# A table of tokens kept in SBUF and filled by matmuls instead of by indirect DMAs, in an attention and mixture-of-experts kernel

## The chip, the cores and the metric

The kernel runs on one core of a Trainium2 chip. The metric is the device time of one execution in microseconds (us), as the median of several runs. The core has a matrix engine, TensorE (PE, with its weight loads shown apart as PEld), and VectorE (DVE), ScalarE (ACT), GpSimd (POOL) and SyncE (SP, which issues most DMAs). Each engine takes its instructions in the order in which the program lists them.

## The reference

Block-causal attention, and then a mixture of experts on its output: each token goes to the expert with the largest logit and its output is scaled by that expert's probability.

```python
def _attn_ref(q, k, v):                       # batch 8, heads 8, seq 576, head_dim 64
    scores = scale * np.matmul(q, k.transpose(0, 1, 3, 2))
    mask = block_i >= block_j                 # blocks of 64 positions
    scores = np.where(mask, scores, -1000000000.0)
    scores = scores - np.max(scores, axis=-1, keepdims=True)
    attn = np.exp(scores)
    attn = attn / (np.sum(attn, axis=-1, keepdims=True) + 1e-09)
    return np.matmul(attn, v)

def _moe_ref(x, expert_emb, tau, w1, w2):     # x: 4608 tokens x 512, 8 experts, hidden 1024
    logits = xn @ en.T / tau                  # rows of x and expert_emb, each over its norm
    expert_idx = np.argmax(logits, axis=1)
    probs = softmax(logits)
    for e in range(E):
        mask = expert_idx == e
        h = np.maximum(x[mask] @ w1[e], 0.0)
        out[mask] = gate_w[mask, None] * (h @ w2[e])
```

## The kernel before, in words

**Attention.** Two heads make a pair; 8 batches of 4 pairs give 32 pairs, `n`. The 576 positions are five row tiles (`NJ` = 5: four of 128 and one of 64). A pair goes through `prep` (transposes of `kn` and `qn`, L326, split into a rounded part `kh`, `qh` and a remainder `kl`, `ql`, L343 and L345), `maxes` (scores for the row maxima, L361 on PE, L367 on DVE; then `nmr`, L374, which PE transposes), `scores` (four matmuls per group, L422, and the exponential on ACT, L429, into `pT` and `pA`; partial row sums on POOL, L400 to L403), `values` (L457), `sums` (L476 to L502, ends in the copy `su`) and `post` (transposes of `oe` and `su`, division, the tokens' rows `xrow` and their logits `lgh`). Several pairs are in flight at once.

**The order of the work** is written out by hand. A string of letters for each pair, in FIRST, STEADY and FINAL, says which part takes its next step: s scores, v values and sums, f post, m maxes, p prep, l loads, r the router. `run()` (L866) reads the string; each letter moves one generator to its next `yield`. So a generator with more steps spreads over more letters, and what follows it comes later. Four PSUM tiles of two banks each (`banks`, L196) go round: `take_bank` takes the one that was given back longest ago, `give_bank` puts one at the end.

**The router.** When a batch's four pairs are done, `route(b)` (L587) finds each token's expert (`ohb`, a one-hot), its rank among the tokens of that expert (matmuls with a triangle of ones, L616 to L620), and for all but the last batch its place in a table of [expert, row of 128 slots, lane]: `table_rows` (L740). The table lies in DRAM. Five indirect DMAs a batch on GpSimd's queue (L672) write 128 token numbers each, 4 bytes to a place:

```python
w = nc.gpsimd.indirect_dma_start(
    out=table, out_offset=bass.IndirectOffsetOnAxis(ap=rowj[:, j:j + 1], axis=0),
    in_=tokf[:, b, j:j + 1], in_offset=None, ...)
```

The table is set to zero at the start by a DMA (L284) and read back by two: `early_rows` (L711) reads the two rows of the early slots when batch 5 (`EB`) is routed, and `tbt` (L1243) reads all of it after the attention part.

**The MoE part** works on slots of 128 tokens of one expert. Weights are streamed and split into rounded part and remainder; each product is three matmuls (L1122). Two early slots of expert 0 begin while the last pairs of attention end (L1238 to L1386): there the four double banks are given up and smaller PSUM pools take their place. `free_bank` (L197) is the double bank that holds the transposed tokens of the early slots, and the new pools are opened in the order `ps_b`, `ps_m1`, `ps_e`.

## Time and profile before

| | |
|---|---|
| median of 3 runs | 811.11 us (809.23 to 811.66) |
| profiled execution | 810.42 us, its span 808.7 us |
| granted TensorE clock | 1.000 of full speed over the span (2.4 GHz) |
| busy share of the span | PE 96%, PEld 78%, DVE 75%, ACT 50%, POOL 54% |
| instructions | PE 7160, DVE 1382, ACT 831, POOL 420 |
| DMA | 93.95 MB in 141421 packets, 118925 of them under 512 bytes |

The span runs from the first instruction to the last; attention fills about the first 350 us, MoE the rest. In a row of the timeline the first number is the start, the second the duration; the bracket at the end says how long the engine had been idle before it and what ended that idle time ("issue": nothing that the profile shows). A row with a count of several instructions gives the time from the first one's start to the last one's end; where matmuls follow each other closely, that includes the latency of the last.

### The profile page before, as it was taken

How to read it: one execution, taken by the hardware profiler on the slowest of the kernel's cores; microseconds unless marked ns; L12 is line 12 of the kernel's file. 1: busy time of each engine (PE TensorE's matmuls, PEld its weight loads, DVE VectorE, ACT ScalarE, POOL GpSimd, SP SyncE). 2: the span in 40 equal slices, each digit the busy share in tenths (PEclk: the TensorE clock that was granted, in tenths of full speed). 3: DMA queues.
4: the chain of work that ended last, by engine and by line, in shares of the span. 5: the costliest groups of instructions: out<-in, count | busy, mean ns of one | idle time of the engine just before them, and what ended most of it. 6: DMA issues, size and time to landing. Idle time of an engine off the chain costs nothing. (4 is left out here: it accounts for less than half of the span.)

```text
span 808.7 us, 23043 instructions
## 1 busy us (share of the span) xinstructions
PE 779.2 (96%) x7160; PEld 627.3 (78%) x7160; DVE 604.2 (75%) x1382; ACT 408.4 (50%) x831; POOL 435.7 (54%) x420
## 2 busy tenths in 40 slices
PE   8999999999999998899999999999999999999997
PEld 3678878787878776668878887788888888888885
DVE  6667878686868776658868777877887778877881
ACT  2566757575757564664744456553533332543222
POOL 7555676767676757772347288784761111661110
PEclk9999999999999999999999999999999999999999
DMA  4745364545454543163845357454441111111111
GB/s 104 169 95 136 84 158 105 147 104 132 101 140 100 141 100 101 29 231 127 297 151 166 100 158 235 152 167 150 148 153 45 55 54 45 38 49 55 54 35 39
DMA packets 141421, 93.95 MB, mean 116 GB/s; under 512 B 118925, under 2 KB 120541, under 8 KB 141260
## 3 DMA queue, kind: packets, MB, share of 16 engines
q1 hardware_dynamic: 133228, 69.74, 31.2%
q0 software_dynamic: 8032, 22.36, 8.7%
q8 instruction: 66, 1.08, 0.6%
q14 instruction: 95, 0.78, 0.3%
HBM read 72.71 MB, written 19.71 MB: 114 GB/s over the span
## 5 line engine op out<-in xcount | busy, mean ns | idle before, releaser
L1175 DVE STREAM_TRANSPOSE pt<-h 32x256 f32<-32x256 f32 x528 | 240.6, 456 | 31.3 <-ACT h L1149 14.1
L367 DVE TENSOR_REDUCE nmx<-psm 128x16 f32<-128x1024 f32 (+2 forms) x128 | 125.6, 986 | 21.4 <-PE psm L361 18.5
L912 POOL TENSOR_TENSOR ring_l<-raw,ring_h 128x1024 f32 (+1 forms) x49 | 116.3, 2406 | 35.7 <-ACT ring_h L907 20.0
L1189 POOL DMA_INDIRECT out_dram<-y,outi x36 | 36.7, 1020 | 176.5 <-ACTq L1061 118.8
L1122 PE MATMUL py<-ring_h,hh 128*128 x272 | 109.3, 402 | 0.7 <-ACT h L1149 0.7
L1122 PE MATMUL py<-ring_l,hh 128*128 x272 | 106.3, 391 | 0.0
L429 ACT ACTIVATE pT<-psm 128x640 f32<-128x640 f32 (+2 forms) x128 | 89.1, 703 | 28.2 <-PE psm L361 16.8
L403 POOL TENSOR_TENSOR pS<-pS,pT 128x640 f32<-128x640 f32 (+2 forms) x93 | 93.5, 1006 | 10.9 <-ACT pT L431 3.2
L1122 PE MATMUL py<-ring_h,hl 128*128 x272 | 88.8, 389 | 0.0
L1122 PE MATMUL ph<-ring_l,xh 128*128 x280 | 86.3, 390 | 0.8 <-POOLq L1073 0.8
L1122 PE MATMUL ph<-ring_h,xh 128*128 x280 | 86.3, 389 | 0.6 <-ACTq L1061 0.6
L457 PE MATMUL psm<-pT,vo 128*64 128x320 f32 (+2 forms) x640 | 76.1, 380 | 1.0 <-issue 1.0
L1188 ACT ACTIVATE y<-py,xg 128x512 f32<-128x512 f32 x34 | 23.4, 689 | 103.5 <-PE py L1122 97.9
L1183 DVE TENSOR_TENSOR hl<-pt,hh 128x512 fp32r<-128x512 f32 x66 | 42.5, 686 | 42.0 <-ACT hh L1181 42.0
L422 PE MATMUL psm<-qh,kh 64*128 64x320 f32 (+4 forms) x384 | 66.5, 341 | 5.9 <-ACT pT L429 3.5
L907 ACT CAST ring_h<-raw 128x1024 f32 (+1 forms) x62 | 61.0, 1050 | 22.1 <-POOLq L1073 11.6
L1181 ACT CAST hh<-pt 128x512 fp32r<-128x512 f32 x66 | 35.5, 590 | 72.1 <-DVE pt L1175 71.7
L1122 PE MATMUL ph<-ring_h,xl 128*128 x280 | 69.2, 389 | 0.0
L457 PEld LDWEIGHTS psm<-pT,vo 128*64 128x64 f32 x640 | 43.2, 137 | 29.3 <-issue 1.9
L1122 PEld LDWEIGHTS ph<-ring_l,xh 128*128 128x128 f32 x280 | 52.5, 188 | 12.1 <-POOLq L1073 1.2
L1122 PEld LDWEIGHTS ph<-ring_h,xh 128*128 128x128 f32 x280 | 52.5, 188 | 11.7 <-ACTq L1061 0.8
L1122 PEld LDWEIGHTS ph<-ring_h,xl 128*128 128x128 f32 x280 | 52.6, 188 | 10.9
(289 smaller groups left out, 1680.7 us busy)
## 6 DMA issues: line engine op xcount, KB each, us to landing
raw<-in_moe_w_dram SPq DMA_DIRECT2D x60, 512.0 KB
qn<-in_q_dram SPq DMA_DIRECT2D x64, 128.0 KB
kn<-in_k_dram SPq DMA_DIRECT2D x64, 128.0 KB
vo<-in_v_dram SPq DMA_DIRECT2D x64, 128.0 KB
xbuf<-xrow SPq DMA_DIRECT2D x28, 260.0 KB
raw<-in_moe_w_dram POOLq DMA_DIRECT2D x4, 512.0 KB
qa<-nmT SPq DMA_DIRECT2D x64, 2.5 KB
xbuf<-xrow SPq DMA_DIRECT2D x7, 130.0 KB
```

Source lines behind the costliest of these rows:

```text
L367: nc.vector.tensor_reduce(m[:, :, f:f + o // w], mt[:, :, 0:o].rearrange("p h (b c) -> p h b c", c=w), axis=AX.X, op=ALU.max, negate=True)
L403: nc.gpsimd.tensor_tensor(o, o, pT[:, :, off[t]:off[t] + w], op=ALU.add)
L422: nc.tensor.matmul(st[0:kw, hh, o:o + c1 - c0], kk[hd[hh], t * P:t * P + kw], qq[hd[hh], 64 + c0:64 + c1], start=(x == 0), stop=(x == len( ...
L429: nc.scalar.activation(pT[:, :, f:f + w] if c0 else pA, st[:, :, 0:w], AF.Exp, scale=scale)
L457: m = nc.tensor.matmul(ob[hh * D:(hh + 1) * D, b0:b0 + q1 - c0], rows(vo, ends_v, n, t)[:, hh, :], pTs[hh][0][:, f0:f0 + q1 - c0] if c0 el ...
L907: return (nc.scalar.copy if eng is nc.scalar else eng.tensor_copy)(piece(ring_h, to, c, half), raw[i][:, c * CW:(c + 1) * CW])
L912: return eng.tensor_tensor(piece(ring_l, to, c, half), raw[i][:, c * CW:(c + 1) * CW], piece(ring_h, to, c, half).bitcast(F32), op=ALU.sub ...
L1122: m = nc.tensor.matmul(out, ac, slots[g]["w", i](r, c * n + off), start=(u == 0 and c == 0), stop=(c == nk - 1 and u == len(turns) - 1))
L1175: nc.vector.transpose(pt[32 * j:32 * j + 32, :, 32 * i:32 * i + 32], h[32 * i:32 * i + 32, :, j, :])
L1181: nc.scalar.copy(sets["hh"][u], pt[:, 4 * u:4 * u + 4])
L1183: nc.vector.tensor_tensor(sets["hl"][u], pt[:, 4 * u:4 * u + 4], sets["hh"][u].bitcast(F32), op=ALU.subtract)
L1189: nc.gpsimd.indirect_dma_start(out=out, out_offset=bass.IndirectOffsetOnAxis(ap=to, axis=0), in_=y, in_offset=None, bounds_check=NT - 1, o ...
```

## The change

The table moves to SBUF as `tbt` [128 lanes, 8 experts, rows], and the indirect DMAs, the zeroing DMA and the two reads of the table go. For each token tile two tables are made: `lane` [128 tokens, 128 lanes], by two ScalarE activations (the square of lane minus the token's lane, then Relu(token - token x square), which leaves the token's number at its lane and 0 elsewhere), and `inrow` [128 tokens, 8 x rows], on GpSimd as the product of the one-hot of the expert and the one-hot of the row. Five matmuls, with `lane` as weights and `inrow` moving, add up in a bank of PSUM, and DVE adds them to `tbt`. The rows counted are `rb` = 5, 9, 14, 18, 23, 27, 32 in batches 0 to 6, so `inrow` is 40 to 256 wide.

For batches 0 to 5 the route begins six router letters later; the subtraction of the largest logit moves from GpSimd to DVE, and the squares for the norms (ACT) are issued among the first router steps. `reserve` is written into `route`. The banks are numbered anew, and at the hand-over the pools are opened in the order `ps_m1`, `ps_e`, `ps_b`; the last pools of the MoE part are opened in another order as well. Four router letters of FINAL's fourth string go, the squares of pairs 29 and 30 are both put off to the end, and the first weight pieces are rounded in turn by GpSimd and ScalarE.

```diff
-    "rfvfsrrrmrrsmrfvfmrrrrsrrmsvmrvvrrvvrrsrrfrfrvfrrrsfvvfrsvvfvvrvrfrr",
+    "rfvfsrrrmrrsmrfvfmrrrrsrrmsvmrvvvvsrrfrfrvfrrrsfvvfrsvvfvvrvrfrr",
...
     banks = [ps_m.tile([P, 2, 512], F32, name=f"psm{i}") for i in range(4)]
-    free_bank = banks[2]
+    banks = [banks[i] for i in (2, 1, 3, 0)]
+    free_bank = banks[0]
...
-        nc.gpsimd.dma_start(table.rearrange("(c p t) o -> p c (t o)", p=RC, t=P),
-                            zcol[0:RC, 0:NCH * P].rearrange("p (c t) -> p c t", t=P))
+        nc.gpsimd.memset(tbt, 0.0)
...
+        def square(j):
+            if b <= EB:
+                squares(xrow[:, j, 0:DM], ss[:, j:j + 1])
+
+        if b <= EB:
+            for _ in range(6):
+                yield
         nc.vector.tensor_reduce(lg, lgh.rearrange("p j h e -> p j e h"), axis=AX.X, op=ALU.add)
         yield
         nc.vector.tensor_reduce(mx, lg, axis=AX.X, op=ALU.max)
         yield
-        eng.tensor_tensor(lg, lg, bc(mx.unsqueeze(2), P, NJ, E), op=ALU.subtract)
+        (nc.vector if b <= EB else eng).tensor_tensor(lg, lg, bc(mx.unsqueeze(2), P, NJ, E), op=ALU.subtract)
...
-            t2 = above(rk, ebase)
+            t2 = sm.tile([P, NJ, E], F32, name="t2")
+            nc.vector.tensor_tensor(t2, rk, ohb, op=ALU.mult)
...
         if b < B - 1:
+            here = inrow[:, :, 0:E * rb]
             for j in range(NJ):
-                w = nc.gpsimd.indirect_dma_start(
-                    out=table, out_offset=bass.IndirectOffsetOnAxis(ap=rowj[:, j:j + 1], axis=0),
-                    in_=tokf[:, b, j:j + 1], in_offset=None, bounds_check=E * RE * P - 1, oob_is_err=False)
...
+                nc.scalar.activation(away, pio, AF.Square, bias=place[:, 0, j:j + 1])
+                nc.gpsimd.tensor_tensor(here[:, j].rearrange("p (e r) -> p e r", e=E),
+                                        bc(ohb[:, j].unsqueeze(2), P, E, rb),
+                                        bc(rowhot[:, j:j + 1, 0:rb], P, E, rb), op=ALU.mult)
+                yield
+                nc.scalar.activation(lane[:, j], away, AF.Relu, bias=tokf[:, b, j:j + 1], scale=tokn[:, b, j:j + 1])
                 if (b == B - 2 or j == NJ - 1) and pieces:
                     store_piece()
                 yield
+            for _ in range(8 if b >= EB else 3):
+                yield
+            bank = take_bank()
+            new = bank[:, 0, 0:E * rb]
+            for j in range(NJ):
+                nc.tensor.matmul(new, lane[:, j], here[:, j], start=(j == 0), stop=(j == NJ - 1))
+            nc.vector.tensor_tensor(tbt[:, :, 0:rb], tbt[:, :, 0:rb], new.rearrange("p (e r) -> p e r", e=E), op=ALU.add)
+            give_bank(bank)
+            yield
...
     def early_rows():
-        et = rt.tile([P, EARLY], F32, name="et")
+        et = tbt[:, 0, 0:EARLY]
         none = rt.tile([P, EARLY], F32, name="enone")
-        nc.sync.dma_start(et, table.rearrange("(p r) o -> p (r o)", p=P)[:, 0:EARLY])
...
-    def table_rows(t, ohb):
+    def table_rows(t, rb):
...
-        nc.gpsimd.tensor_tensor(t, t, ohb, op=ALU.mult)
+        rowt = sm.tile([P, 2, NJ], I32, name="rowt")
+        place = sm.tile([P, 2, NJ], F32, name="place")
         yield
         nc.vector.tensor_reduce(rowj, t, axis=AX.X, op=ALU.max)
         yield
...
+        nc.vector.tensor_scalar(place, rowt, -1.0, None, op0=ALU.mult)
+        nc.vector.tensor_tensor(rowhot[:, :, 0:rb], bc(minus[:, 0:rb].unsqueeze(1), P, NJ, rb),
+                                bc(place[:, 1].unsqueeze(2), P, NJ, rb), op=ALU.is_equal)
...
     ring(0)
-    tbt = st.tile([P, NCH * RC], F32, name="tbt")
-    nc.sync.dma_start(tbt, table.rearrange("(p r) o -> p (r o)", p=P))
...
     banks.remove(free_bank)
+    banks[1:] = banks[:0:-1]
...
+    ps_m = pool(psum_t, "ps_m1", 4, space=PSUM, reuse_waits="tile")
+    ps_e = pool(psum_t, "ps_e", 1, space=PSUM, reuse_waits="tile")
     ps_b = pool(psum_t, "ps_b", 1, space=PSUM, reuse_waits="tile")
-    ps_m = pool(psum_t, "ps_m1", 4, space=PSUM, reuse_waits="tile")
```

How this moves instructions is seen in the order on single engines. In the names, `psm_147` to `psm_153` are the double banks of PSUM; a number names one tile within one kernel only, here and for `kh`, `qh`, `kl`, `ql`, `qa` and `pT`. The lines L326 to L502 of before are seven higher after the change. The first place is PE in the pair after a batch has been routed. Before, the 320-wide scores follow the last maxes and take the bank of the earlier 320-wide scores (psm_152), whose exponential is done:

```order
L422 MATMUL psm_150<-qh_183,kh_189 128x448 x2
L422 MATMUL psm_150<-ql_186,kh_189 128x448 x2
L422 MATMUL psm_150<-qh_183,kl_192 128x448 x2
L422 MATMUL psm_150<-qa_195,ka 128x448 x2
L361 MATMUL psm_151<-kh_190,qh_184 128x64 x2
L422 MATMUL psm_152<-qh_183,kh_189 128x320 x2
L422 MATMUL psm_152<-ql_186,kh_189 128x320 x2
L422 MATMUL psm_152<-qh_183,kl_192 128x320 x2
L422 MATMUL psm_152<-qa_195,ka 128x320 x2
L326 MATMUL psm_153<-ident,kn_157 128x64 x8
```

After, the five lane matmuls stand between:

```order
L429 MATMUL psm_149<-qh_180,kl_189 128x448 x2
L429 MATMUL psm_149<-qa_192,ka 128x448 x2
L711 MATMUL psm_148<-inrow,lane 128x144 x5
L368 MATMUL psm_150<-kh_187,qh_181 128x64 x2
L429 MATMUL psm_147<-qh_180,kh_186 128x320 x2
L429 MATMUL psm_147<-ql_183,kh_186 128x320 x2
L429 MATMUL psm_147<-qh_180,kl_189 128x320 x2
L429 MATMUL psm_147<-qa_192,ka 128x320 x2
L333 MATMUL psm_148<-ident,kn_154 128x64 x8
```

They take a bank of the round (psm_148), the maxes behind them the next one (psm_150), and the 320-wide scores the bank that was used by the earlier maxes of 192 and 320 columns (psm_147), which DVE reduces.

The second place is ACT in the same pair. Before, the cast of `kh` and one exponential lie between the 448-wide exponential and the copy of the sums:

```order
L429 ACTIVATE pA<-psm_152 128x512
L429 ACTIVATE pT_212<-psm_153 128x2x320
L429 ACTIVATE pT_212<-psm_152 128x2x448
L343 CAST kh_190<-psm_151 128x2x5x64
L429 ACTIVATE pT_212<-psm_153 128x2x320
L502 COPY su_206<-psm_150 128x192
L379 CAST nmT<-psm_153 10x128
L429 ACTIVATE pT_212<-psm_152 128x2x192
```

After, the lane tables of the batch stand among them:

```order
L702 ACTIVATE lane<-away,tokf,tokn 128x128
L697 ACTIVATE away<-pio,place 128x128
L436 ACTIVATE pT_217<-psm_148 128x2x448
L702 ACTIVATE lane<-away,tokf,tokn 128x128
L350 CAST kh_186<-psm_149 128x2x5x64
L697 ACTIVATE away<-pio,place 128x128
L436 ACTIVATE pT_217<-psm_150 128x2x320
L702 ACTIVATE lane<-away,tokf,tokn 128x128
L697 ACTIVATE away<-pio,place 128x128
L509 COPY su_202<-psm_147 128x192
L386 CAST nmT<-psm_150 10x128
L436 ACTIVATE pT_217<-psm_148 128x2x192
```

Between the cast of `kh` and the copy `su` there are three more activations of 128x128, and three more ahead of the cast.

The third place is DVE in the pair in which a batch's route begins. Before, the first router steps stand ahead of the `ql` subtraction (L345) and among the reductions of the maxes (L367):

```order
L594 TENSOR_REDUCE lg<-lgh 128x40
L596 TENSOR_REDUCE mx<-lg 128x5
L345 TENSOR_TENSOR ql_186<-psm_150,qh_183 128x2x5x64
L601 SCALAR_TENSOR_TENSOR t_2116<-lg,erev 128x40
L367 TENSOR_REDUCE nmx_200<-psm_153 128x2x8
L371 MEMSET nmx_200 64x2x2
L603 TENSOR_REDUCE mx<-t_2116 128x5
L367 TENSOR_REDUCE nmx_200<-psm_150 128x2x8
L371 MEMSET nmx_200 64x2x2
L605 TENSOR_TENSOR hot_110<-t_2116,mx 128x40
L367 TENSOR_REDUCE nmx_200<-psm_153 128x2
L607 MEMSET hot_110 64x4
```

After, four of them stand together behind the last of these reductions and ahead of `nmr` (L374, after the change L381):

```order
L374 TENSOR_REDUCE nmx_197<-psm_148 128x2x8
L378 MEMSET nmx_197 64x2x2
L374 TENSOR_REDUCE nmx_197<-psm_147 128x2
L611 TENSOR_REDUCE lg<-lgh 128x40
L613 TENSOR_REDUCE mx<-lg 128x5
L615 TENSOR_TENSOR lg<-lg,mx 128x40
L618 SCALAR_TENSOR_TENSOR t_2889<-lg,erev 128x40
L381 TENSOR_REDUCE nmr_199<-nmx_197 128x10
```

The subtraction `lg<-lg,mx` is a DVE instruction now; before, it stood in POOL's queue.

## Rows read from the trace of the kernel before

**Rows 1.** The page: busy us (share of span) x instructions, by engine
```profile
PE 779.2 (96%) x7160; PEld 627.3 (78%) x7160; DVE 604.2 (75%) x1382; ACT 408.4 (50%) x831; POOL 435.7 (54%) x420
```

**Rows 2.** Windows: us, busy us (instructions) of PE, PEld, DVE, ACT, POOL; clock, DMA, GB/s
```profile
700.00:750.00 50.00, 50.00 (x231) 41.38 (x230) 40.51 (x85) 18.73 (x36) 21.94 (x16) 1.00 0.17 53
```

**Rows 3.** Groups of instructions by line and shape: busy us, mean ns, idle before
```profile
L672 POOL DMA_INDIRECT table<-tokf,rowj x35 | 35.2, 1005 | 9.9 <-issue 9.5 <-ACT oe L463 0.2
...
L400 POOL TENSOR_TENSOR pS<-pA,pT 128x256 f32<-128x256 f32 x31 | 22.7, 732 | 65.4 <-ACT pT L429 65.4
...
L582 ACT ACTIVATE xs<-xrow 128x128 f32<-128x128 f32 x20 | 6.2, 311 | 2.6 <-DVE xrow L538 2.1
```

**Rows 4.** Timeline, batch 2's route: start, duration, instruction, idle before and its releaser
```profile
183.52 0.42 PE L361 MATMUL psm<-kh,qh 64*128 64x192 f32 x4
...
184.25 0.47 PE L422 MATMUL psm<-qh,kh 64*128 64x448 f32 x2 [0.31 <-issue]
...
184.91 0.97 POOL L672 DMA_INDIRECT table<-tokf,rowj  x1 [0.30 <-issue]
...
185.86 1.55 DVE L367 TENSOR_REDUCE nmx<-psm 128x16 f32<-128x1024 f32 x2 [1.93 <-PE psm L361]
...
185.87 0.41 PE L422 MATMUL psm<-qh,kh 64*128 64x320 f32 x2 [0.52 <-ACT pT L429]
...
187.14 0.47 PE L326 MATMUL psm<-ident,kn 64*128 64x64 f32 x8 [0.43 <-DVE nmx L367]
```

**Rows 5.** Timeline, PE: first transposes of `kn` in three more pairs
```profile
175.88 0.40 PE L326 MATMUL psm<-ident,kn 64*128 64x64 f32 x8
...
197.44 0.46 PE L326 MATMUL psm<-ident,kn 64*128 64x64 f32 x8 [0.30 <-DVE nmx L367]
...
207.37 0.46 PE L326 MATMUL psm<-ident,kn 64*128 64x64 f32 x8 [0.19 <-DVE nmx L367]
```

**Rows 6.** Timeline of the pair before batch 3's route, four instructions
```profile
194.91 2.48 DVE L367 TENSOR_REDUCE nmx<-psm 128x16 f32<-128x1024 f32 x2
...
196.31 0.39 PE L422 MATMUL psm<-qh,kh 64*128 64x320 f32 x2
...
199.19 0.33 ACT L502 COPY su<-psm 128x192 f32<-128x192 f32 x1
...
199.65 0.29 PE L326 MATMUL psm<-ident,su 64*128 64x64 f32 x4
```

**Rows 7.** Timeline, router steps of two batches with the sums on POOL
```profile
207.36 0.19 DVE L605 TENSOR_TENSOR hot<-t,mx 128x40 bf16<-128x40 f32 x1
...
207.95 0.24 PE L619 MATMUL psm<-hot,onesb 128*128 128x32 bf16 x4
...
208.27 1.58 POOL L401 TENSOR_TENSOR pS<-pT 128x640 f32<-128x640 f32 x1
...
209.80 0.27 PE L326 MATMUL psm<-ident,nmr 64*128 64x64 f32 x2
...
336.26 1.54 POOL L401 TENSOR_TENSOR pS<-pT 128x640 f32<-128x640 f32 x1
...
336.64 1.23 DVE L605 TENSOR_TENSOR hot<-t,mx 128x40 bf16<-128x40 f32 x1
```

**Rows 8.** Timeline, PE: end of the attention part and the early slots
```profile
308.52 0.55 PE L457 MATMUL psm<-pT,vo 128*64 128x192 f32 x4 [0.96 <-issue]
...
311.12 0.50 PE L361 MATMUL psm<-kh,qh 64*128 64x448 f32 x4 [1.03 <-issue]
...
338.05 0.19 PE L616 MATMUL psm<-hot,triS 128*128 128x40 bf16 x1 [0.93 <-DVE hot L607]
...
347.61 0.48 PE L422 MATMUL psm<-qh,kh 64*128 64x448 f32 x2
...
349.61 0.34 PE L326 MATMUL psm<-ident,su 64*128 64x64 f32 x4
...
360.05 0.50 PE L1122 MATMUL psm<-ring_h,xh 128*128 128x512 f32 x1 [0.79 <-DVE hl L1101]
```

More of the change, by code (lines that the diff above doesn't have):

```diff
@@ L628, in route @@
             give_bank(rb)
+        square(4)
         yield
@@ L653, in route @@
         if b < B - 1:
-            rowj = yield from table_rows(t2, ohb)
+            rb = -(-(b + 1) * S // P)
+            place = yield from table_rows(t2, rb)
         nc.vector.reciprocal(ss, ss)
@@ L685 @@
     early_g = []
-    writes, ends = [], []
+    ends = []
     ei = st.tile([P, 2, EARLY], I32, name="ei")
@@ L1279 @@
     split_lo(0, 3, 0)
-    late.pop()()
+    for f in late:
+        f()
     for c in range(NPC):
```

65 lines of the change are left out of this document (32 added, 33 removed).

## The prediction

> **What bounds the kernel now.** I read the busy shares first: TensorE (PE) is busy 96% of the span, VectorE (DVE) 75%, ScalarE (ACT) 50%, GpSimd (POOL) 54% [rows 1]. In the MoE part PE has no idle time, 50.00 of 50 us [rows 2], so nothing can be won there but by taking PE work away, and the change touches none of it. What can move is the attention part, where PE stops for short waits; each counts in full if no later wait shrinks with it. So I looked, in the timeline of single instructions, for PE waits near what the diff removes, then for the slack of the instructions beside which it puts new work.
>
> What goes is 35 indirect DMAs, each 1.0 us of GpSimd [rows 3]. GpSimd has room, so that time is worth nothing by itself. But around the issues PE waits, though its producers are done. In batch 2's route the maxes of L361 start at 183.52 and last 0.42, so they end at 183.94; the reduction of them on DVE starts at 185.86 and its row names those maxes as releaser of a 1.93 wait. PE stands 0.31 ahead of the 448-wide scores (releaser "issue"), 0.52 ahead of the 320-wide ones, 0.43 ahead of the `kn` transposes: 1.26 in all, while POOL issues these DMAs, the last of the three from 184.91 to 185.88 [rows 4]. From `kn` to `kn` that pair takes 187.14 - 175.88 = 11.26 us, the next 197.44 - 187.14 = 10.30, the one after 207.37 - 197.44 = 9.93 [rows 4, 5]. I read this as: while such a DMA is issued, signals between the other engines come late.
>
> **The change part by part**, against the profiled execution's own 810.42 us (0.7 below the median of the runs, 811.11).
>
> *Removed DMAs, batches 0 to 4.* Bounds per batch: nothing, if other waits fill the holes, and 1.7 (both pairs over the undisturbed 9.93: 1.33 + 0.37). The waits say 1.26, the neighbouring pair 0.96. I take 1.1: 5 x 1.1 = 5.5 us gained.
>
> *Batch 5.* Two waits with releaser "issue", 0.96 at 308.52 and 1.03 at 311.12 [rows 8], go: 2.0 (bounds 0 and 2.0).
>
> *Batch 6*, the last with a table, issues its five while little runs. The last 448-wide score group stretches from 347.61 to 349.61, 2.00 us [rows 8]; four streams of 448 columns at the rate of 512 in 50/231 = 0.216 [rows 2] are 4 x 0.19 = 0.76. So 1.2, and 0.7 for the rest of its five issues, at 1.1/5 each: 1.9 (bounds 0 and 2.6).
>
> *PSUM of the early slots.* At 360.05 PE waits 0.79 for a DVE subtraction that reads `free_bank` [rows 8]: the new pool of maxes' tiles begins on that bank. With the new order a bank that was free longer lies there: 0.8 (0 to 0.8). What is late next is the loaded weight half, which I can't see there; hence the lower end.
>
> *The one-hot's wait.* At 338.05 the rank matmuls wait 0.93 for the one-hot [rows 8], because its DVE operation took 1.23 instead of 0.19 and ended when the sum on POOL that ran since 336.26 ended [rows 7]. Batch 6 keeps its order, with other neighbours: I take half, 0.5 (0 to 0.9).
>
> Gains: 5.5 + 2.0 + 1.9 + 0.8 + 0.5 = 10.7.
>
> *Products on POOL.* 35 products of 40 to 256 elements. L400, 256 elements wide, takes 0.73 [rows 3]; so they are shorter than the 1.0 of the DMA each replaces. POOL gets lighter: 0.
>
> *Lane matmuls.* 7 x 5 on PE, which hides nothing. Nearest below: four 128-row matmuls of 32 to 8 columns together 0.24 [rows 7]; nearest above: 512 columns, 0.216 each [rows 2]. So between 0.24 and 1.08 a batch. With 40 to 256 columns I take 0.3. They also take a bank out of the round of four. As the order shows, the 320-wide scores behind them then need a bank that the reductions from 194.91 to 197.39 still hold, while today they start at 196.31 [rows 6]: 1.1 later, less the 0.30 that `kn` waits today [rows 5], the matmuls themselves and the earlier maxes. I add 0.2: 7 x 0.5 = 3.5 (bounds 7 x 0.24 = 1.7 and 7 x (1.08 + 0.8) = 13).
>
> *Lane tables on ACT.* 70 activations of 128x128. One of that shape takes 0.31 [rows 3]; they overlap, so 0.2 to 0.3 each, 14 to 22 us on an engine half idle. It costs where ACT's next output is wanted: the copy `su` ends at 199.52 and PE transposes it at 199.65 [rows 6], a slack of 0.13. Three activations are put ahead of it: 3 x 0.2 - 0.13 = 0.45 on five batches, 2.25 (bounds 0 and 5 x 0.8 = 4.0).
>
> *Router later, subtraction on DVE.* Four DVE operations now stand ahead of `nmr`, whose transposes PE starts at 209.80 [rows 7]. The subtraction and the product behind it read two operands in SBUF. If they meet L400 and L401 on POOL, as the one-hot met one at 336.64, they wait for its end: up to 208.27 + 1.58 = 209.85 [rows 7], and `nmr` follows some 0.4 later (two short operations such as the 0.19 at 207.36), against 209.80 today. Against that, the `ql` subtraction no longer has router work ahead of it, and `kn` waits 0.19 to 0.30 for that chain today [rows 5]. Between -0.3 and +2.1 a batch; I take 0.3, x 6 = 1.8.
>
> The remaining edits (the zeroing DMA, the reads of the table, the one gather later, the squares among router steps, `split_hi` on other engines) lie beside PE work; without that cover each is one wait of at most about 1 us. Taken as 0.
>
> Sum: 810.4 - 10.7 + 3.5 + 2.25 + 1.8 = 807.3; I state **807.2**.
>
> **The rivals.**
>
> *A: the new work hides.* For it: ACT and POOL are half idle [rows 1], and between the last lane table and its matmuls lie three to eight further steps of the plan. Then only the streams are paid, 7 x 0.3 = 2.1: 810.4 - 10.7 + 2.1 = 801.8. Against it: the slack of 0.13 ahead of `su`, and the round of four banks that is full.
>
> *B: slower, by POOL holding up DVE.* At 336.64 a DVE operation on two SBUF operands waited until the POOL sum was over [rows 7]. If the subtraction passes between L400 and L401 and the product that depends on it then waits the whole of L401, 1.58, `nmr` and with it PE wait in six batches: (1.58 - 0.3) x 6 = 7.7, giving 815.0. It decides from the point where the subtraction is not over before L400 starts, 0.73 ahead of L401 [rows 3]. Against it: POOL no longer issues DMAs, so L400 may stand elsewhere in the next batches, and the DVE queue may pass earlier. The Trainium skill, in "SBUF — State Buffer", section "SBUF: two separate sides", has this as a rule: a DVE instruction with two SBUF inputs and a GpSimd instruction share a port pair, and whichever starts first keeps the pair for its whole instruction. The 1.23 against 0.19 agrees [rows 7]; by that rule every new DVE operation with two SBUF operands, and each of the 35 products, is a possible further wait, and the result would be the 815.0 of this rival.
>
> *C: no change.* The waits at the issues shrink only to what is late next: of the 1.26, the 0.52 names an exponential on ACT, the 0.43 a DVE reduction [rows 4]; both engines get more work. With half of the 10.7 kept and the costs as above: 810.4 - 5.3 + 7.5 = 812.6; with ACT's part hidden, 810.3. Middle 811.
>
> That the change doesn't do what it says I exclude: the order holds no table DMA any more.
>
> **How the numbers follow.** Forecast 0.47 (own range 804.0 to 810.0: the large terms off by a quarter each), A 0.20, B 0.15, C 0.18. The range that leaves out about 2 in 10 takes in A's 801.8 nearly whole and C, but not B: 801.0 to 812.8. A measurement of this kernel tells about 0.3%, 2.4 us, from no change. Faster by more: A, and four fifths of the forecast's share: 0.20 + 0.38 + 0.02 from C = 0.60. Slower: B, and a little of C: 0.17. Within: 0.23.
>
> **What would show it.** Right: from `kn` to `kn` the pairs with the lane tables take about 10.5 instead of 11.3, no wait with releaser "issue" above 0.2 in the attention part, no 0.79 where the early slots' first layer starts. The costs: a wait on ACT `su` of about 0.45, one on a DVE reduction ahead of the 320-wide scores, lane matmuls of about 0.06 each. Wrong: if waits on `nmr` of over 1 us stand in each router pair (B); if the pairs keep their 11 us with other releasers (C); if lane tables cost no wait at all (A); if the issue waits were not of the DMAs, the 1.26 stays where no indirect DMA runs.

## The result, and the profile after

The changed kernel is slower by 1.2%, clear of the scatter: 819.75 us (median of 6 runs, 818.39 to 820.77) against 810.22 (6 runs, 809.17 to 811.66), a ratio of 1.0116 with a 95% interval of 1.0099 to 1.0133. The forecast was 807.2, with a range of 801.0 to 812.8. The profiled execution took 820.77 us, its span 819.1, at a mean clock of 0.991. It is the longest of the six; the mean clock differs from one execution to the next, and the times follow it: 818.39 us at 0.996, 819.49 to 819.92 at 0.994, 820.59 and 820.77 at 0.989 and 0.991.

The page's first row shows little of it: PE is busy for 3.8 us more than in [rows 1], in a span that is 10.4 us longer.

```profile
PE 783.0 (96%) x7195; PEld 634.3 (77%) x7195; DVE 618.4 (76%) x1403; ACT 434.4 (53%) x901; POOL 410.9 (50%) x407
```

So I cut both spans at the same points of the program: where a pair's `kn` transposes start (pair n is the stretch from the n-th to the next), and where PE's last matmul ends.

| stretch | before, us | after, us | difference |
|---|---|---|---|
| start to pair 7 | 73.31 | 73.32 | 0.01 |
| pairs 7 to 27 (five routes and the start of batch 5's) | 217.57 | 219.83 | +2.26 |
| pair 28 (one-hot of batch 5, after the change) | 13.64 | 19.44 | +5.80 |
| pairs 29 and 30 | 19.76 | 17.66 | -2.10 |
| last `kn` to PE's last matmul (batch 6, MoE) | 479.08 | 477.88 | -1.20 |
| PE's last matmul to the end of the span | 5.34 | 10.92 | +5.58 |
| sum | 808.71 | 819.05 | +10.35 |

**A batch in the middle.** Before, four pairs took 9.93, 10.27, 11.27 and 10.28 us: 41.75. After, 9.51, 11.17, 9.51 and 11.86: 42.05. The starts after the change, as the timeline of PE has them:

```profile
199.49 0.28 PE L333 MATMUL psm<-ident,kn 64*128 64x64 f32 x4
...
209.00 0.40 PE L333 MATMUL psm<-ident,kn 64*128 64x64 f32 x8
...
220.17 0.28 PE L333 MATMUL psm<-ident,kn 64*128 64x64 f32 x4
...
229.68 0.22 PE L333 MATMUL psm<-ident,kn 64*128 64x64 f32 x2
...
241.54 0.22 PE L333 MATMUL psm<-ident,kn 64*128 64x64 f32 x2
```

No wait at an "issue" is left, and the waits of `kn` of [rows 5] are gone too. Three others stand there instead. The first, in the pair in which the route begins, on POOL, DVE and PE:

```profile
210.04 0.27 DVE L615 TENSOR_TENSOR lg<-lg,mx 128x40 f32<-128x40 f32 x1
...
210.20 1.55 POOL L408 TENSOR_TENSOR pS<-pT 128x640 f32<-128x640 f32 x1
...
210.34 1.47 DVE L618 SCALAR_TENSOR_TENSOR t<-lg,erev 128x40 f32<-128x40 f32 x1
...
211.74 0.21 DVE L381 TENSOR_REDUCE nmr<-nmx 128x10 f32<-128x70 f32 x1
...
212.10 0.28 PE L333 MATMUL psm<-ident,nmr 64*128 64x64 f32 x2 [0.90 <-DVE nmr L381]
```

The subtraction L615 ends at 210.31; the product behind it, L618, lasts 1.47 and ends at 211.81, just behind the POOL sum that ends at 211.75; `nmr` comes after it, and PE waits 0.90. The groups by line show the same over the whole kernel. Before:

```profile
L601 DVE SCALAR_TENSOR_TENSOR t<-lg,erev 128x40 f32<-128x40 f32 x8 | 2.1, 257 | 0.4 <-POOL lg L598 0.4
```

After:

```profile
L618 DVE SCALAR_TENSOR_TENSOR t<-lg,erev 128x40 f32<-128x40 f32 x8 | 9.2, 1152 | 0.6 <-POOL lg L615 0.4
```

The same instruction takes 1152 ns in the mean instead of 257. The rule of the Trainium skill quoted under rival B ("SBUF — State Buffer", "SBUF: two separate sides") agrees: the product on two SBUF operands lost to a GpSimd sum that had started 0.14 earlier.

The other two, in the pair of the lane tables, on ACT and PE:

```profile
231.16 0.41 ACT L697 ACTIVATE away<-pio,place 128x128 f32<-128x128 f32 x1
...
231.46 0.70 ACT L436 ACTIVATE pT<-psm 128x640 f32<-128x640 f32 x1
...
232.04 0.49 ACT L702 ACTIVATE lane<-away,tokf,tokn 128x128 fp32r<-128x128 f32 x1
...
232.21 0.27 PE L333 MATMUL psm<-ident,nmr 64*128 64x64 f32 x2 [0.34 <-ACT pT L436]
...
232.57 0.40 ACT L697 ACTIVATE away<-pio,place 128x128 f32<-128x128 f32 x1
...
232.88 0.30 ACT L509 COPY su<-psm 128x192 f32<-128x192 f32 x1
...
233.23 0.34 PE L333 MATMUL psm<-ident,su 64*128 64x64 f32 x4 [0.74 <-ACT su L509]
```

There is one tile `away`, and a `lane` that reads it does not overlap with the next `away` that writes it: from 232.04 to 232.57 are 0.53, while the copy `su` starts 0.31 behind the `away` ahead of it. PE waits 0.34 ahead of `nmr` and 0.74 for `su`. The mean durations are 404 and 487 ns, where I had taken 0.2 apiece from an activation of the same shape [rows 3]:

```profile
L702 ACT ACTIVATE lane<-away,tokf,tokn 128x128 fp32r<-128x128 f32 x35 | 17.0, 487 | 0.3
L697 ACT ACTIVATE away<-pio,place 128x128 f32<-128x128 f32 x35 | 14.1, 404 | 0.6
```

The five lane matmuls stand in the same pair. The pair before it has the same scores around that place without them:

```profile
228.78 0.37 PE L429 MATMUL psm<-qa,ka 64*128 64x448 f32 x2
...
229.01 0.39 PE L429 MATMUL psm<-qh,kh 64*128 64x320 f32 x2
...
239.74 0.37 PE L429 MATMUL psm<-qa,ka 64*128 64x448 f32 x2
...
240.03 0.78 PE L711 MATMUL psm<-inrow,lane 128*128 128x144 f32 x5
...
240.88 0.39 PE L429 MATMUL psm<-qh,kh 64*128 64x320 f32 x2
```

From the last 448-wide scores to the first 320-wide ones are 0.23 without and 1.14 with them, so they cost 0.91 here, and the trace names no wait for a bank at that place. Over the seven batches, 40 to 256 columns wide, the time from the first of the five to the next instruction is 0.66 to 0.75: the width hardly matters.

**Pair 28.** The timeline of DVE and PE around batch 5's one-hot, then three windows (columns as in [rows 2]):

```profile
298.62 0.19 DVE L624 TENSOR_TENSOR hot<-t,mx 128x40 bf16<-128x40 f32 x1
298.72 1.22 DVE L374 TENSOR_REDUCE nmx<-psm 128x2 f32<-128x1024 f32 x1
...
300.00 0.06 DVE L627 MEMSET hot<- 64x4 uint32 x1
...
300.11 0.19 PE L637 MATMUL psm<-hot,triS 128*128 128x40 bf16 x1 [1.93 <-DVE hot L627]
...
300.83 4.53 PE L464 MATMUL psm<-pT,vo 128*64 128x128 f32 x20
```

```profile
296.00:300.00 4.00, 1.95 (x26) 1.38 (x27) 3.66 (x13) 3.37 (x10) 3.05 (x4) 0.98 0.14 32
300.00:304.00 4.00, 3.60 (x23) 1.93 (x24) 3.03 (x15) 0.58 (x3) 1.43 (x2) 0.50 0.47 106
304.00:308.00 4.00, 4.00 (x46) 3.23 (x46) 0.62 (x2) 1.61 (x3) 0.25 (x1) 0.67 0.29 66
```

PE stands idle for 1.93 us, since the memset that completes the one-hot is queued behind a reduction of 1.22. Then the granted clock is 0.50, the level of 1.2 GHz: twenty matmuls of the values take 4.53. Ahead of `nmr` the pair has the wait of the steady batches too, 0.88 at 296.23. Before, the same rank matmuls stood elsewhere (291.44) and waited for nothing.

**The end.** PE's last matmul ends at 808.14, the last output DMA is issued at 809.14, and then nothing runs for 9 us:

```profile
809.14 0.99 POOL L1214 DMA_INDIRECT out_dram<-y,outi  x1 [4.43 <-POOLq L1489]
...
810.00:815.00 5.00, 0.00 (x0) 0.00 (x0) 0.00 (x0) 0.00 (x0) 0.13 (x1) 0.68 0.07 26
```

The sequencers' records, which the rows above leave out, say what the span waits for: GpSimd's closing drain runs from 811.38 to 818.23, 6.85 us; before, from 805.33 to 807.88, 2.54. The record ahead of it in the same queue (INC_SWDGE_SEM) takes 1.84 instead of 0.52. These two, 4.31 and 1.32, make up the 5.58 but for 0.05.

### The profile page after: what moved, and what is told of

Read it like the earlier page. It is cut to its first block, busy times and chain, and to the rows that moved or that the text cites. A ratio compares the mean times of both kernels' runs of the same rounds, so it can differ in the third digit from the quotient of the medians.

```text
span 819.1 us, 23114 instructions
## 1 busy us (share of the span) xinstructions
PE 783.0 (96%) x7195; PEld 634.3 (77%) x7195; DVE 618.4 (76%) x1403; ACT 434.4 (53%) x901; POOL 410.9 (50%) x407
## 5 line engine op out<-in xcount | busy, mean ns | idle before, releaser
L374 DVE TENSOR_REDUCE nmx<-psm 128x16 f32<-128x1024 f32 (+2 forms) x128 | 125.8, 986 | 17.0 <-PE psm L368 13.8
L464 PE MATMUL psm<-pT,vo 128*64 128x320 f32 (+2 forms) x640 | 77.9, 388 | 0.0
L407 POOL TENSOR_TENSOR pS<-pA,pT 128x256 f32<-128x256 f32 x31 | 22.8, 734 | 106.3 <-ACT pT L436 106.2
```

What stands on the lines that cost most here:

```text
L374: nc.vector.tensor_reduce(m[:, :, f:f + o // w], mt[:, :, 0:o].rearrange("p h (b c) -> p h b c", c=w), axis=AX.X, op=ALU.max, negate=True)
L464: m = nc.tensor.matmul(ob[hh * D:(hh + 1) * D, b0:b0 + q1 - c0], rows(vo, ends_v, n, t)[:, hh, :], pTs[hh][0][:, f0:f0 + q1 - c0] if c0 el ...
```

## The experiments

Pairs, waits and tail below are from the trace of each run. "Tail" is the time from PE's last matmul to the end. The jobs ran on several chips, each with the kernel before beside it.

**Where does the loss of pair 28 come from?** `eb_early`:

```diff
-        if b <= EB:
+        if b < EB:
             for _ in range(6):
                 yield
```

> The changed kernel, but batch 5's route begins six letters earlier again, as before the change (batches 0 to 4 keep the delay). Theory: the delay put batch 5's one-hot so late that PE waited 1.93 us for it, and the TensorE clock then fell to 1.2 GHz; that place cost 19.44 - 13.64 = 5.8 us. Without it: no wait on the one-hot over 0.5 us, clock 1.00 up to 350 us, and the time falls by 4 to 6, to 814 to 816. Rival: the stall comes from the other work that was added there (squares, lane tables, order of the banks); then the wait stays somewhere in that pair and the time stays within 1.5 of 819.75.

Measured: 821.24 us (1.0146, 1.0125 to 1.0167). The wait of 1.93 and the fall of the clock at 300 were gone, and pairs 27 to 30 took 44.15 instead of 46.61. But the stretch behind them grew from 477.88 to 480.43: PE waits 0.78 for `kh` in it, and the clock falls behind the wait for `oe`, which the changed kernel has as well (1.74 at 351.11).

```profile
349.50 0.30 PE L500 MATMUL psm<-oe,enT 128*32 128x128 f32 x2 [1.74 <-ACT oe L470]
...
352.00:356.00 4.00, 3.93 (x44) 3.51 (x45) 1.98 (x8) 2.40 (x5) 0.07 (x1) 0.69 0.15 55
```

The profiled execution of the changed kernel has no such fall, but the change of place did not make it: `after_again` below is the unchanged changed kernel, and there the clock falls behind the same wait (0.69 in 352 to 356). So the wait went, the saving did not come.

`eb_fill`, the same wait filled with work:

```diff
+        if b == EB:
+            for _ in range(9):
+                nc.tensor.matmul(rb[:, 1], onesb, bc(onesb.unsqueeze(1), P, 512 // P, P), start=True, stop=True)
         nc.tensor.matmul(rk, triS, ohb, start=True, stop=False)
```

> The changed kernel with nine 512-wide dummy matmuls (about 2 us of PE work, into a half of the rank bank that is overwritten) ahead of batch 5's rank matmuls: PE works through the time in which it waited. Theory: the idle time of 1.93 us is what brought the clock down; with the fill the clock stays at 1.00 and the 20 matmuls of the values after it take 2.3 us instead of 4.53; the clock's part of the loss is 2.8, so about 817.0, and the wait's part stays. Rival: the clock falls for another reason (the waits before, or not by idleness); then it falls again and the time is 819.7 or a little more.

Measured: 818.06 us (1.0096, 1.0082 to 1.0110). The clock stayed up and the twenty matmuls took 2.38:

```profile
298.52 2.10 PE L639 MATMUL psm<-onesb 128*128 128x512 bf16 x9 [0.56 <-DVE lgh L552]
...
301.16 2.38 PE L464 MATMUL psm<-pT,vo 128*64 128x128 f32 x20
...
300.00:304.00 4.00, 3.71 (x40) 2.40 (x40) 2.64 (x13) 0.67 (x2) 1.43 (x2) 1.00 0.44 98
```

Pair 28 went from 19.44 to 17.22; later the clock fell, to 0.50 in 352 to 356. But that the fill kept it up at 300 is not shown, since one execution stands against one, and others with the same wait of 1.93, unfilled, went otherwise. In `after_again` the clock is low for a shorter time, and pair 28 takes 17.93; in `after_dma15`, whose code is that of the changed kernel from batch 3 on, it does not fall, and pair 28 takes 16.66. Below, the first three lines are of `after_dma15`, the last two of `after_again`:

```profile
299.79 0.18 PE L640 MATMUL psm<-hot,triS 128*128 128x40 bf16 x1 [1.93 <-DVE hot L630]
...
300.49 2.38 PE L467 MATMUL psm<-pT,vo 128*64 128x128 f32 x20
...
300.00:304.00 4.00, 3.71 (x51) 2.67 (x49) 3.02 (x14) 1.07 (x3) 1.61 (x3) 1.00 0.42 96
...
300.00:304.00 4.00, 3.70 (x25) 2.09 (x26) 3.03 (x14) 0.48 (x3) 1.44 (x2) 0.59 0.44 101
...
352.00:356.00 4.00, 3.94 (x44) 3.51 (x45) 1.98 (x8) 2.38 (x5) 0.69 (x4) 0.69 0.36 134
```

So of the 5.80 us of pair 28 in the profiled execution, 2.78 are the clock's (19.44 - 16.66), and the other 3.02 are, to 0.2, the two waits of 0.88 and 1.93. With the clock up, pairs 27 to 30 take 43.84 in `after_dma15`, 44.15 in `eb_early` and 44.41 here, against 43.33 before: neither the earlier place nor the fill won anything there but the clock. The times say the same: at a mean clock of 0.995 or 0.996 the changed kernel took 817.15 (in `after_again`) and 818.39, `eb_fill` 817.62 to 818.30, `eb_early` 819.77.

**Is it POOL's sum that delays `nmr`?** `nmr7`:

```diff
-            for _ in range(6):
+            for _ in range(7 if b < EB else 6):
                 yield
```

> The changed kernel with seven instead of six letters of delay in batches 0 to 4: of DVE's instructions the product of the router (L618) then stands behind nmr instead of ahead of it; lg, mx and the subtraction still stand ahead. Theory (rival B of the prediction): L618 waits for the end of the POOL sum L408 (1.47 us instead of 0.19), and nmr behind it; with L618 behind nmr the wait of 0.90 ahead of the nmr transposes goes in five batches, 5 x 0.9 = 4.5: about 815.3. Rival: the four operations as such are too much ahead of nmr (lg alone takes 0.74), or L618 behind nmr holds up kl in the same way; then the wait of 0.9 stays or reappears at kl, and the time is 819 to 820.

Measured: 824.00 us (1.0167, 1.0151 to 1.0183), slower still. In the pair aimed at the wait is gone: `nmr` runs at 211.51, while the sum L408 runs. But everything in the route is one step later, and a batch takes 43.1 us: PE waits 1.19 for the one-hot late in the same pair and 1.00 ahead of the next `nmr`.

```profile
211.49 1.56 POOL L408 TENSOR_TENSOR pS<-pT 128x640 f32<-128x640 f32 x1
211.51 0.21 DVE L381 TENSOR_REDUCE nmr<-nmx 128x10 f32<-128x70 f32 x1
...
218.11 0.18 PE L637 MATMUL psm<-hot,triS 128*128 128x40 bf16 x1 [1.19 <-DVE hot L627]
...
224.61 0.28 PE L333 MATMUL psm<-ident,nmr 64*128 64x64 f32 x2 [1.00 <-DVE nmr L381]
```

The mechanism is shown; the price of 0.9 a batch is read from the wait, and from pair 20, which takes 11.17 instead of 10.27. That moving the step wins it back was wrong.

`no_late` takes the delay away altogether:

```diff
-        if b <= EB:
-            for _ in range(6):
-                yield
```

> The changed kernel without the six letters of delay in batches 0 to 5; the subtraction stays on DVE and the squares stay among the first router steps. Theory: the router's product is then no longer ahead of nmr while the POOL sum runs, so the wait of 0.90 ahead of nmr goes and the kn waits of 0.2 to 0.3 come back; the wait of 1.93 on batch 5's one-hot goes, and with it the fall of the clock there. The lane tables stand six letters earlier and keep their 1.1 a batch somewhere. 6 x 0.6 = 3.6 in the pairs, and about 2.5 in batch 5: 813 to 816. Rival: as with one letter more, the waits only move to other places in the pairs; then 819 to 822.

Measured: 824.90 us, with batches of 42.7 (10.10, 11.50, 10.48, 10.65) and waits of 0.51 ahead of `nmr`, 0.57 for `su` and 0.40 and 0.30 for `kn`. Pair 28 takes 18.20 here too, with a wait of 1.96 ahead of `nmr` and a fall of the clock behind it. The rival held: the delay that I held against the change is better than none, and batch 5 loses without it as well.

**What do the lane tables on ACT cost?** `lane_pool`:

```diff
-                nc.scalar.activation(away, pio, AF.Square, bias=place[:, 0, j:j + 1])
...
-                nc.scalar.activation(lane[:, j], away, AF.Relu, bias=tokf[:, b, j:j + 1], scale=tokn[:, b, j:j + 1])
+                nc.gpsimd.tensor_scalar(lane[:, j], pio, place[:, 0, j:j + 1], tokf[:, b, j:j + 1],
+                                        op0=ALU.is_equal, op1=ALU.mult)
```

> The changed kernel with the lane tables made by GpSimd, one operation of 128x128 a tile (compare with the lane, times the token number), instead of by two ScalarE activations. Theory: the activations ahead of su and of the exponentials cost 0.74 + 0.34 in the pair after each route, and 1.74 + 0.37 in batch 6; without them six batches give 1.08 back and batch 6 about 2: 8 less the 0.3 of slack, so 811.5 to 813. Rival: GpSimd takes the place of ScalarE (35 more operations of about 0.4 us ahead of its sums, whose results PE transposes or multiplies); then waits on pS appear and the time stays above 817.

Measured: 817.94 us (1.0095, 1.0081 to 1.0109). The pair of the lane tables fell from 11.86 to 10.6 to 11.4, and pairs 7 to 27 by 4.1 in all (215.7 against 219.83), less than the 5 x 1.08 = 5.4 expected, since the lane matmuls now wait for their tables; 0.95 ahead of `nmr` stayed. Batch 6 took it back: GpSimd needs 796 ns for a table, and the matmuls wait 3.5 us for the last ones.

```profile
L698 POOL TENSOR_SCALAR lane<-pio,place,tokf 128x128 fp32r<-128x128 f32 x35 | 27.9, 796 | 0.0
...
L707 PE MATMUL psm<-inrow,lane 128*128 128x256 f32 x5 | 1.9, 385 | 3.5 <-POOL lane L698 3.5
```

`mixm`: lane tables on GpSimd up to batch 5, on VectorE in batch 6, and the memset moved:

```diff
+                (nc.gpsimd if b <= EB else nc.vector).tensor_scalar(lane[:, j], pio, ...)
...
         nc.vector.tensor_tensor(ohb, t1, bc(mx.unsqueeze(2), P, NJ, E), op=ALU.is_equal)
         square(2)
-        yield
+        if b != EB:
+            yield
         nc.vector.memset(ohb[64:P, NJ - 1, :], 0.0)
```

> The changed kernel with three waits taken away: the lane tables are made by GpSimd in batches 0 to 5 (as in lane_pool) and by VectorE in batch 6 (compare with the lane, times the token number), and batch 5's memset of the one-hot stands right behind the comparison instead of behind a 1.22 us reduction of the maxes. Theory: lane_pool's batches took 41.25 us against 42.10, so 5 x 0.85 = 4.2; the wait of 1.74 for oe in batch 6 goes without lane_pool's 3.5 on the lane matmuls; the wait of 1.93 falls to about 0.7 and the clock stays at 2.4 GHz (2.2 to 2.8 of eb_fill and of the half-speed values). About 819.6 - 4.2 - 1.7 - 4 = 809.7. Rival: as in eb_early the saved time is lost again at the next wait (nmx, oe, second fall of the clock near 350 us); 815 or more.

Measured: 813.19 us (811.83 to 814.12), between the two. The tables' waits are gone, and the wait for `oe` too; PE's last matmul ends at 800.74, 7.4 earlier than after the change (6.1 earlier than in `after_again`). The one-hot still costs 0.79, a second wait of 1.06 comes behind it, and the clock falls all the same (0.57 in 296 to 300); in `mixm_dma15` below, with the same two waits, it does not.

```profile
294.76 0.18 PE L637 MATMUL psm<-hot,triS 128*128 128x40 bf16 x1 [0.79 <-DVE hot L625]
...
296.12 0.17 PE L647 MATMUL psm<-hot,onesb 128*128 128x6 bf16 x1 [1.06 <-DVE t L644]
```

**The indirect DMAs and the end.** `before_nodma`, run three times, and `after_dma` go opposite ways:

```diff
-                w = nc.gpsimd.indirect_dma_start(out=table, ...)       # before_nodma
...
+                w = nc.gpsimd.indirect_dma_start(                      # after_dma
+                    out=table, out_offset=bass.IndirectOffsetOnAxis(ap=dmai[:, k:k + 1], axis=0),
+                    in_=tokf[:, b, j:j + 1], in_offset=None, ...)
```

> The changed kernel with the 35 indirect DMAs issued again at their old places in the router (128 token numbers each, to a DRAM table that nobody reads), beside the lane tables and matmuls. Two questions. First the end: the changed kernel's span goes on for 10.9 us after PE's last matmul, before 5.3, because GpSimd's closing drain takes 6.85 instead of 2.5. Theory: the length of that drain hangs on how many software DMAs were issued before; with the 35 back it is about 2.5 again and the tail 5.3, 5.6 less. Rival: it comes from the other new work on GpSimd (35 products, one memset); then the tail stays 10.9. Second the attention part: with the issues back, PE should wait again near them (0.3 'issue', 0.5 for the exponential), about 1.1 a batch on top of the waits for nmr and su. With both: 819.75 - 5.6 + 5.5 + 2 = about 821.5; with the tail alone 814; by the rival 826.

> The kernel before without its 35 indirect DMAs; every other step is kept. The table stays zero, so the gathers and the output writes of the MoE part move no rows of batches 0 to 6 (that part of the computation is left out); PE's work is unchanged. Theory: the waits at the issues were caused by the DMAs: the pair with three of them falls from 11.26 us (from kn to kn) to about 10.1, the one with two from 10.30 to 9.9, a batch from 41.75 to about 40.5, and the waits of 0.96 and 1.03 in batch 5 go; attention ends 7 to 9 us earlier. Rival: the waits are of that place in the pair whatever GpSimd does; then the pairs keep 11.3 and 10.3. The end: if the closing drain hangs on the number of software DMAs, the tail is 10.9 us instead of 5.3.

Measured: `after_dma` 884.47 us with a tail of 5.51 (drain 2.38); `before_nodma` 797.84 with a tail of 11.38 (drain 7.03), beside a kernel before of 793.88. So the tail follows the DMAs that GpSimd issues (software DMAs), not the new work. The attention part could not be read from either. In `after_dma` the score matmuls waited for the DMA of `qa`:

```profile
115.94 0.76 PE L432 MATMUL psm<-qa,ka 64*128 64x256 f32 x2 [4.02 <-DMA qa<-nmT]
```

And on that chip, as its 793.88 us say, the kernel before can hardly have the waits at the issues. No trace of it is from there; the next run, which issues all 35 DMAs, comes nearest: `before_psum`.

```diff
+    banks = [banks[i] for i in (2, 1, 3, 0)]
...
+    ps_m = pool(psum_t, "ps_m1", 4, space=PSUM, reuse_waits="tile")
+    ps_e = pool(psum_t, "ps_e", 1, space=PSUM, reuse_waits="tile")
     ps_b = pool(psum_t, "ps_b", 1, space=PSUM, reuse_waits="tile")
```

> The kernel before with only the PSUM part of the change: the four banks numbered anew, the pools at the hand-over opened in the new order, and the last pools too. Theory: of before's waits only the 0.79 at the early slots' first layer goes, 0.8: 809.4. Rival: the banks' new numbers change which bank waits for which reduction all over attention, and the hand-over waits elsewhere; then the pairs' lengths change, by up to 2 us in either direction.

Measured: 795.11 us against 793.88 (1.0027, 1.0012 to 1.0043): a little slower. Its pairs with DMAs take 9.51 to 9.56, without them 9.88 and 10.25 as before, and `before_nodma` has the same to 0.05.

`before_again` and `after_again`, both unchanged:

> The kernel before, unchanged, profiled again, because the job that ran before_psum and no_late gave 793.88 us for it and the two jobs before gave 810.2. In the trace of before_psum the pairs with indirect DMAs take 9.51 us, in the first trace of before 11.26 and 10.30, and no other pair differs by more than 0.1. Theory: what an indirect DMA's issue costs the other engines differs from chip to chip: about 810 with pairs of 11.3 and 10.3, or about 794 with pairs of 9.5, nothing between. Rival: it is the PSUM part that removes the waits; then this trace has 11.3 and 10.3 whatever the time is.

> The changed kernel, unchanged, on the same chip as the kernel before. It issues no indirect DMA in the router, so by the theory that only their price differs between chips it takes about 819.7 here too, with pairs of 11.16, 9.51, 11.85 and 9.52 and a tail of 10.9; against 794 that would be 3.2% slower, against 810 1.2%. Rival: the chips differ in more than that; then the changed kernel too falls to about 803 where before takes 794.

Measured on one chip: 810.51 and 819.59 us, beside 811.65. `before_again` has pairs of 11.21 and 10.25 from batch 2 on; `after_again` has 11.17, 9.51, 11.84 and 9.52 and a tail of 10.92. So there are chips of two kinds for the kernel before, 16 us apart. The changed kernel itself has no run on the faster kind; the nearest is `after_dma15` below, 819.29 on a chip where the kernel before takes 793.68, with the pairs of `after_again` to 0.05 in batches 1 to 4. So on that kind the change costs about 3%.

`after_dma2` and `after_dma5` issue 35 and 5 DMAs with places 1 KB apart, `after_dma15` and `mixm_dma15` 15:

> The changed kernel with the 35 indirect DMAs issued again, as in the run after_dma, but with places 1 KB apart instead of 4 bytes (in after_dma the score matmuls waited 4.0 us for the DMA of qa, which I put down to 128 neighbouring words of DRAM). Theory: the tail is 5.3 to 5.5 instead of 10.9; the attention part gets 0 to 2.5 us a batch longer, by the chip: 814 where before takes 794, up to 829 where it takes 810. Rival: the waits for qa return with these places too (then they come from the issues among the lane tables); 860 or more.

> The same with only batch 0's five indirect DMAs. Does the tail go with the number of software DMAs (10.9 - 5.6 x 5/35, about 10.1), or is there a number from which it is short (then 10.9 or 5.3)? By the first the time is about 819, by a threshold that five reach 814.5.

> The changed kernel with only the same 15 indirect DMAs. If the drain counts them as above, the tail falls from 10.9 to 3.3 to 4 and the pairs stay as they are (after_dma2 had 9.49 and 11.86 with them): 819.6 - 7 = 812.6. If it falls evenly: 818.4; if it steps down to 2.4: 814.2.

> The same with 15 indirect DMAs more (batches 0 to 2, to a table nobody reads). Only the end should change: the closing drain was 6.85 with none, 7.26 with five and 2.38 with 35, which fits 0.08 us for each software DMA since a point that is passed again at about ten more. Then with 15 it is about 0.7 and the tail 3.3 to 4: 7 less than mixm. Rival: the drain falls evenly with the number (then 5.6, tail 9.7) or steps down to 2.4 (tail 5.5).

| run | software DMAs added | us | closing drain | tail |
|---|---|---|---|---|
| after (after_again and six other runs have the same drain and tail) | 0 | 819.75 | 6.85 | 10.92 |
| after_dma5 | 5 | 821.33 | 7.26 | 11.41 |
| after_dma15 | 15 | 819.29 | 8.08 | 12.44 |
| mixm_dma15 | 15 | 835.96 | 8.08 | 12.44 |
| after_dma2 | 35 | 824.20 | 2.38 | 5.51 |

The drain grows by 0.082 us for each software DMA, (8.08 - 6.85)/15, and drops between 15 and 35 more; my guess that it drops at about ten was wrong. What makes it drop was not tried. In `mixm_dma15` the lane tables on GpSimd stood behind the DMAs, and PE waited 1.8 to 2.1 twice for them in each of the three batches. In `after_dma2` the waits for `qa` are gone, so they most likely came with the places 4 bytes apart, though `after_dma` ran on another chip. It gave another surprise: on the chip on which `before_again` waits at the issues its pairs stayed 11.16, 9.51, 11.9 and 9.50 in most batches, with no wait named "issue". The DMAs were not free all the same: the pair with the lane tables of batch 4 takes 14.15 instead of 11.90, a wait of 1.25 for `inrow` stands in batch 6, and PE's last matmul ends at 816.60, 8.5 later than without them, so the short tail won nothing.

`before_nodma_2` and `before_nodma_3` were to settle the price of the DMAs, and both fell on chips of the other kind:

> The kernel before without its 35 indirect DMAs, once more (rows of batches 0 to 6 are not moved in the MoE part; PE's work is the same), for a chip on which the kernel before takes 810. Its first run was on a chip on which before took 794 and the pairs with DMAs 9.5 us, so it could tell nothing of the waits at the issues. Theory: these DMAs make the waits, on some chips only; then the pairs are 9.5 here too instead of 11.2 and 10.3, attention ends 15 to 17 us earlier, and with a tail of 11.4 the time is about 800. Rival: the waits belong to that place in the pair on such a chip; then the pairs stay 11.2 and 10.3 and the time is about 816 (after_dma2 showed no such waits with all 35 DMAs in the changed kernel, which speaks for this).

> The kernel before without its 35 indirect DMAs, a third time, since both runs so far fell on chips on which before takes 794 (rows of batches 0 to 6 are not moved in the MoE part). On a chip on which before takes 810: if the DMAs make the waits there, pairs of 9.5 instead of 11.2 and 10.3 and about 798 as on the other chips; if chip and place make them, pairs of 11.2 and 10.3 and about 815. On a chip of the other kind 798 again, and the question stays open.

Measured: 798.00 and 797.73 us beside 793.68 and 794.76, with pairs of 9.51, a tail of 11.38: inconclusive for the price, and a third and fourth witness, after `before_nodma` and `after_dma`, for the tail. The last run, `before_const`, writes to fixed places of a second table:

```diff
-                    out=table, out_offset=bass.IndirectOffsetOnAxis(ap=rowj[:, j:j + 1], axis=0),
+                    out=table2, out_offset=bass.IndirectOffsetOnAxis(ap=dmai[:, b * NJ + j:b * NJ + j + 1], axis=0),
```

> The kernel before with its 35 indirect DMAs in their places, but with fixed places 1 KB apart in a second table that nobody reads, instead of the places that the router computed (so the table read stays zero and rows of batches 0 to 6 are not moved in the MoE part). The three jobs with a kernel without these DMAs all had the kernel before at 794, the three others at 810 to 812. If before takes 810 here: pairs of 11.2 and 10.3 mean that any such issue at this place makes PE wait, pairs of 9.5 that the computed places do (after_dma2 had no such waits with fixed places). If before takes 794 here, pairs of 9.5 follow from the chip, and its being fast has nothing to do with a kernel without the DMAs beside it. In both cases the tail is 5.3, since 35 software DMAs are there.

Measured: 808.98 us beside 811.28, pairs of 11.25 and 10.31, and the three waits of [rows 4] to 0.02:

```profile
182.71 0.47 PE L425 MATMUL psm<-qh,kh 64*128 64x448 f32 x2 [0.30 <-issue]
...
184.34 0.41 PE L425 MATMUL psm<-qh,kh 64*128 64x320 f32 x2 [0.54 <-ACT pT L432]
...
185.62 0.46 PE L329 MATMUL psm<-ident,kn 64*128 64x64 f32 x8 [0.42 <-DVE nmx L370]
```

So on such a chip the waits stand in the kernel before whatever places the DMAs write; the computed table has no part in it. Its tail is 4.67 and its drain 1.92, where I expected 5.3: with 35 DMAs too the drain differs a little.

No version beat the kernel before: the best of the changed ones, `mixm`, has 813.19 us, and it was run only beside a kernel before of 793.68.

## Why the prediction was wrong

The direction failed. The step that weighs most is one that I had costed at nothing; most of the others were sized wrongly.

*"The remaining edits ... taken as 0", the end.* I summed only up to PE's last matmul, and priced the 35 DMAs only where they are issued. The 5.58 us behind it are GpSimd's closing drain and the record ahead of it, both longer with the 35 DMAs gone; `before_nodma` and `after_dma` show it from both sides. This is more than half of the 9.5 us. Nothing in [rows 1 to 8] was of that stretch.

*Batch 5.* The two "issue" waits of [rows 8] did go, and pair 29 is 2.4 shorter (9.18 for 11.59), as I had counted. But I looked at the six letters of delay only where the plan is the steady one, ahead of `nmr`, and took 0.3 for it. In the plan of the last pairs the same delay puts the one-hot behind a reduction of 1.22, and waits of 0.88 and 1.93 eat up the gain: pairs 27 to 30 take 0.5 more than before even with the clock up (`after_dma15`), where my terms gave 1.2 less. In the profiled execution they take 3.3 more, and 2.8 of that is a fall of the clock, which I had not thought of. The fall comes and goes from one execution to the next; by the six executions it is worth about 1.4 us in the median (819.75 - 818.39), an estimate. The delay alone is not the cause: without it `eb_early` and `no_late` wait elsewhere in these pairs.

*Removed DMAs.* 1.1 a batch was too little for a chip like the first: its DMA pairs take 11.27 + 10.28 us, on the other chips 9.51 + 9.51, so 2.5 a batch, above my upper bound of 1.7. On the other chips it is nothing. Why the chips differ, and why the DMAs of `after_dma2` cost next to nothing in the pairs of the first batches even on the first kind, stays open. That the DMAs are the cause on such a chip is not shown by taking them away there; it is likely, since nearly all of the pairs that are longer there than in `before_psum` are those in which they are issued. Against it speaks `after_dma2`.

*Lane tables.* The mechanism was right, the size was not: 0.74 + 0.34 a batch instead of 0.45, because the activations on the one tile `away` don't overlap. `lane_pool` gave 4.1 back over the pairs. In batch 6, which I had left out, five tables ahead of `oe` made PE wait 1.74; in `mixm`, with the tables on other engines, that wait is gone.

*`nmr`.* This is rival B: 0.90 a batch instead of 0.3. I had its mechanism, place and deciding instant, and gave it 0.15. It went as rival B says: the subtraction is over only when the sum L408 has begun, and the product waits for the whole of it.

*Lane matmuls.* Under-priced: 0.5 a batch, where a steady batch shows 0.91. The bank's part was not there, as the 320-wide scores wait for no bank after the change; the matmuls' own part was 0.3 and is over 0.6 at every width. The four bf16 matmuls of 32 to 8 columns that I took as the nearest below [rows 7] were no measure for these.

*PSUM.* The wait of 0.79 is gone after the change; a wait of 0.51 for `su` stands near it in `eb_early` and `nmr7`, and alone, in `before_psum`, the edit gained nothing.

*Batch 6.* I had 3.2 gained (issues, PSUM, one-hot) and 0.5 lost; 1.2 came. The waits of 0.79 and of 0.93 for the one-hot are gone, and the 448-wide scores take 1.34 to the next transposes instead of 2.00; the wait for `oe` (1.74 for 0.36) and the lane matmuls took most of it back.

Put together, the steady batches went as the sum goes (+0.3 a batch, where I had +0.15), by errors that cancel: more gained (2.5 at the DMAs) and more lost (0.9 for `nmr`, 1.1 for the tables, 0.9 for the lane matmuls) than I had. That is luck. The end decided; without it the change would still be some 4 us slower, by batch 5 and its clock, by the gains that batch 6 did not keep, and by the steady batches.

## What to carry to other kernels

Follow a moved step through every plan that it runs in, the last iterations first: there the queues are others, and the clock may fall behind a wait of 2 us. Sum up to the end of the span, not of the busiest engine: what a change takes off a queue can come back in what closes the kernel. And a wait that one step of delay takes away must be looked for one step later: `nmr7`, `no_late` and `eb_early` each removed or shortened the wait that they aimed at, and none got faster. Last, before a difference between two traces is given to an edit, look at the unchanged kernel's other executions: here the clock alone makes 2.8 us in one pair.

## What the runs showed of the hardware

The kernel before took 793.7 to 794.8 us on three chips and 810 to 812 on two (the chip of the first runs is not known). Against `before_psum`, a run on the faster kind, nearly all of the difference that I found, 14 of 16 us, is in pairs in which GpSimd issues indirect DMAs. GpSimd's closing drain takes 0.082 us longer for each software DMA added, from 6.85 to 8.08 over 15, and 1.92 to 2.54 where all 35 are issued. PE's clock fell behind a wait of 1.93 in `after`, `after_again` and four more runs and stayed at 1.00 behind the same wait in `after_dma15`; behind the wait of 1.74 for `oe` it stayed at 1.00 in `after`, `after_dma5` and `after_dma15` and fell in `after_again`, `eb_early` and `eb_fill`. It did not fall after waits of 0.96 and 1.03 [rows 8]. What tells these apart, no run shows.
